# An attention and token-mixer kernel on one core: the first chunk of rows normalised in two halves, v's products of two row blocks first, and identity turns on TensorE until rows arrive

## The chip, the cores and the metric

The kernel runs on one core of one Trainium2 chip. Its engines are TensorE (PE in the profile; PEld is its loading of weights), VectorE (DVE), ScalarE (ACT), GpSimd (POOL) and SyncE (SP), which here issues nearly all DMAs. The metric is the time of one execution on the device in microseconds (us), as the median over runs; lower is better.

## The reference, cut to what matters

`x` has 2048 rows of 512 columns. It is normalised along its rows twice: once for attention, and once more inside the token mixer.

```python
xn = _layernorm(x)
s = _A_ref(xn, A_wqkv, A_wo)                  # 32 heads of 16
g = _silu(_B_ref(xn, B_w1, B_b1, B_w2, B_b2))
return x + s * g

# _A_ref: qkv = x @ wqkv; p = softmax(q k^T * 16 ** -0.5); o = p v; o @ wo
# _B_ref: h = layernorm(x); u = gelu(h^T w1 + b1); y = u w2 + b2; y^T
```

All inputs are float32.

## The kernel before, in words

**Stages.** A first stage normalises x, makes q, k and v, and stores them in DRAM (`q_d`, `k_d`, `v_d`). It takes about 150 us. The rest of the 1700 us goes over the pairs of heads with scores, maxima, exponentials and values, with the mixer's matmuls filled in between. The change lies in the first stage.

**Precision.** Every operand of a matmul is split into an upper part (a copy rounded to `float32r`) and a lower part (the operand less its upper part), and a product is made of three matmuls: upper by upper, upper by lower, lower by upper. The upper part is a copy on ACT, the lower part a subtraction (`sub`, line L79) on DVE where the operand comes out of PSUM, and on POOL for weights and for the second normalisation.

**The first stage.** The 2048 rows are four chunks of four blocks of 128 rows. For a chunk c:

- `load_x` (L165) loads four row blocks; `first(c)` makes a `Norm`: for each block `stats` (L205, L206), then one `rsqrt` for all four (L212 to L218, with the square root on ACT at L213 and one Newton step on DVE), then `apply` for each block (L222), which writes `xn`.
- `turned(c, db)` (L268) transposes column block db of all four row blocks on PE, as a product with the identity `ident`; ACT copies the upper part into `xt` (L270), DVE subtracts for the lower part.
- q and k: eight groups of twelve matmuls (L303), with the weights as the stationary operand and the turned rows moving. ACT copies the upper part of each result (L308) into `sg`, DVE makes the lower part, and SP stores it. Pieces of the next chunk's first normalisation and of this chunk's `second` normalisation (for the mixer, `hx` and `hu`) are put between the groups, in the list `todo`.
- v: for the chunk's four row blocks, twelve matmuls each (L86 to L88), between which the next chunk's rows are turned. ACT copies the result into `v48` (L357), where every head has its 16 columns and 16 ones, and SP stores it (L358).

**Order.** The program's order is written out by hand; each engine takes its instructions in that order, and waits on semaphores are put in from the tiles used. `bank()` hands out the eight PSUM banks in turn. The `xt` tiles come from the pool `pt`, six buffers of one turned column block each.

**Weights.** `wqkv` is loaded in twelve pieces of 128 rows and 512 columns (L185), q's four first, then k's, then v's. There are eleven buffers, so the tenth piece waits until the first is split. `w_upper` (L190) copies the upper parts on ACT, `w_lower` subtracts on POOL. A one-column copy on POOL, `hold` (L280), reads `xn[3]`, so that POOL begins its subtractions when the first chunk's four blocks are normalised.

**Start of the kernel.** The first chunk's normalisation stands alone, with nothing else for PE; the mixer's biases `b1` and `b2` are loaded behind chunk 1's rows (L292, L293), and DVE halves the second (`b2h`, L294) ahead of its work on chunk 0's first q group.

Of the kernel before, what the change touches and what calls it, by code (L numbers as in the profile page):

```python
# [8 lines left out]
F32 = mybir.dt.float32  # L9
F32R = mybir.dt.float32r  # L10
AF = mybir.ActivationFunctionType
OP = mybir.AluOpType
# [9 lines left out]
def tile_attention_token_mixer(ctx, tc, x, wqkv, wo, w1, b1, w2, b2, out):  # L22
    nc = tc.nc
    P = 128
    S, D = x.shape
    F = w1.shape[1]
    DH = 16
    H = D // DH
    NP = H // 2
    NB = S // P  # L30
    ND = D // P
    NF = F // P
    NC = S // 512
# [23 lines left out]
    v_d = dram.tile([NB, P, NP * 48], F32, name="v_d")  # L57
# [6 lines left out]
    ident = const.tile([P, P], F32, name="ident")  # L64
# [13 lines left out]
    def sub(eng, o, a, b):  # L78
        eng.tensor_tensor(out=o, in0=a, in1=b.bitcast(F32), op=OP.subtract)  # L79
# [74 lines left out]
    with (  # L154
        tc.tile_pool(name="pw", bufs=1) as pw,
        tc.tile_pool(name="px", bufs=5) as px,
        tc.tile_pool(name="pt", bufs=6) as pt,
        tc.tile_pool(name="pst", bufs=3) as pst,
    ):
        xr, xn = {}, {}  # L160
# [27 lines left out]
        def w_upper(part):  # L188
            for kd in range(ND):
                nc.scalar.copy(wh[part][:, kd, :], raw_w[part, kd])  # L190

        def w_lower(part):
            for kd in range(ND):
                sub(nc.gpsimd, wl[part][:, kd, :], raw_w[part, kd], wh[part][:, kd, :])

        class Norm:


            def __init__(self, src, dst, then=None):
                self.src, self.dst, self.then = src, dst, then  # L200
# [5 lines left out]
                nc.vector.bn_aggr(self.mv[:, b, :], self.st[:, b, :])  # L206

            def rsqrt(self):
                ve = pst.tile([P, 4], F32, name="ve")
                r = self.r = pst.tile([P, 4], F32, name="r")  # L210
                t = pst.tile([P, 4], F32, name="t")
                nc.vector.tensor_scalar(ve, self.mv[:, :, 1], 1e-5, None, op0=OP.add)  # L212
                nc.scalar.sqrt(t, ve)  # L213
                nc.vector.reciprocal(r, t)
                nc.vector.tensor_tensor(out=t, in0=r, in1=r, op=OP.mult)
                nc.vector.tensor_tensor(out=t, in0=t, in1=ve, op=OP.mult)
                nc.vector.tensor_scalar(t, t, -0.5, 1.5, op0=OP.mult, op1=OP.add)
                nc.vector.tensor_tensor(out=r, in0=r, in1=t, op=OP.mult)  # L218
# [8 lines left out]
                    self.then(b, o)  # L227

            def pieces(self):
                for b in range(4):  # L230
                    yield lambda b=b: self.stats(b)
                yield self.rsqrt
                for b in range(4):
                    yield lambda b=b: self.apply(b)

        def first(c):
# [4 lines left out]
            return Norm(lambda b: xr[4 * c + b], dst)  # L241

        def second(c):
            def then(b, o):
# [8 lines left out]
        def bank():  # L253

            i = turn_of[0] = (turn_of[0] + 1) % 8
            pl, nm = ((ps_sc, "sc"), (ps_mx, "mx"), (ps_dn, "dn"), (ps_av, "av"))[i % 2 if i < 6 else i - 4]
            return pl.tile([P, 512], F32, name=nm)

        for f in first(0).pieces():
            f()  # L260
        w_upper(0)
        xts_ = [[] for _ in range(NC)]

        def turned(c, db):

            ps = bank()
            for b in range(4):
                nc.tensor.transpose(ps[:, b * P : (b + 1) * P], xn[4 * c + b][:, db * P : (db + 1) * P], ident)  # L268
            t = pt.tile([P, 2, 512], F32R, name="xt")
            nc.scalar.copy(t[:, 0, :], ps)  # L270
            sub(nc.vector, t[:, 1, :], ps, t[:, 0, :])
            xts_[c].append(t)

        for c in range(NC):
            cs = slice(c * 512, (c + 1) * 512)
            for db in range(len(xts_[c]), ND):
                turned(c, db)
            if c == 0:

                nc.gpsimd.tensor_copy(pst.tile([P, 1], F32, name="hold"), xn[3][:, :1])  # L280
                w_upper(1)
                w_lower(0)
                w_lower(1)
            xt = xts_[c]
            todo = []
            if c + 1 < NC:
                load_x(c + 1)
                todo += list(first(c + 1).pieces())
            if c == 0:
                w_upper(2)  # L290
                w_lower(2)
                nc.sync.dma_start(b1t, b1.rearrange("(b p) -> p b", p=P))  # L292
                nc.sync.dma_start(b2t, b2.rearrange("(b p) -> p b", p=P))  # L293
                nc.vector.tensor_scalar(b2h, b2t, 0.5, None, op0=OP.mult)  # L294
            todo += list(second(c).pieces())
            order = [(part, g) for part in range(2) for g in range(ND)]
            per = -(-len(todo) // (len(order) + 2))
            for n, (part, g) in enumerate(order):
                m = slice(g * P, (g + 1) * P)
                ps = bank()  # L300
                for w, z in ((wh, 0), (wh, 1), (wl, 0)):
                    for kd in range(ND):
                        nc.tensor.matmul(  # L303
                            ps, w[part][:, kd, m], xt[kd][:, z, :],
                            start=w is wh and z == 0 and kd == 0, stop=w is wl and kd == ND - 1,
                        )
# [33 lines left out]
            pv = [bank()[:, :D] for _ in range(4)]  # L340
            if c + 1 < NC:
                for kd in range(ND):
                    for b in range(4):
# [3 lines left out]
            for b, ps in enumerate(pv):  # L347
                if c + 1 == NC:
                    for kd in range(ND):
                        v_product(b, kd)  # L350
                if c + 1 < NC or b < 2:
                    v48 = pst.tile([P, NP, 3, DH], F32, name="v48", bufs=2)
                else:
                    v48 = pt.tile([P, 2, 512], F32R, name="xt").bitcast(F32).rearrange("p a b -> p (a b)")
                    v48 = v48[:, : NP * 48].rearrange("p (a b c) -> p a b c", b=3, c=DH)
                nc.gpsimd.memset(v48[:, :, 1, :], 1.0)
                nc.scalar.copy(v48[:, :, 0:3:2, :], ps.rearrange("p (a b c) -> p a b c", b=2, c=DH))  # L357
                nc.sync.dma_start(v_d[4 * c + b], v48.rearrange("p a b c -> p (a b c)"))  # L358


    vpp = pool("vp", 2, reuse_waits="tile")
# [689 lines left out]
    ps = two()  # L1051
# [50 lines left out]
```

## Time and profile before

| | us |
|---|---|
| median of 3 runs | 1701.65 |
| lowest and highest | 1699.56, 1702.52 |
| the profiled execution | 1699.51 |
| its span, first to last instruction | 1697.7 |

The prediction below shows lines of the profile. A line of the timeline has the start of an instruction in us from the span's start, how long it took (merged if xN says so), engine, source line, operation, what it writes and reads, its shape, and in brackets how long the engine was idle before it and what ended that. PE rows end in a modelled time, so successive starts tell more than durations. A line of the waits has the waiting instruction, what it waited for, us in total, times, and the longest. A line of the windows has the stretch, its length, the busy time of PE, PEld, DVE, ACT and POOL (with instructions), the granted TensorE clock, the DMA engines' busy share and GB/s.

### The profile page before, as it was taken

How to read it: one execution, taken by the hardware profiler on the slowest of the kernel's cores; microseconds unless marked ns; L12 is line 12 of the kernel's file. 1: busy time of each engine (PE TensorE's matmuls, PEld its weight loads, DVE VectorE, ACT ScalarE, POOL GpSimd, SP SyncE). 2: the span in 40 equal slices, each digit the busy share in tenths (PEclk: the TensorE clock that was granted, in tenths of full speed). 3: DMA queues.
4: the chain of work that ended last, by engine and by line, in shares of the span. 5: the costliest groups of instructions: out<-in, count | busy, mean ns of one | idle time of the engine just before them, and what ended most of it. 6: DMA issues, size and time to landing. Idle time of an engine off the chain costs nothing.

```text
span 1697.7 us, 30716 instructions
## 1 busy us (share of the span) xinstructions
PE 1662.0 (98%) x11693; PEld 842.7 (50%) x11693; DVE 1425.0 (84%) x2476; ACT 1188.0 (70%) x2292; POOL 566.5 (33%) x671
## 2 busy tenths in 40 slices
PE   7999999999999999989999999999999999999997
PEld 6887644444444444444444444444444444444443
DVE  6655998888888888878888888888889988889845
ACT  3332277777777777767777777777777777787764
POOL 3223843234342344323322322222222222372411
PEclk9999999999999999999999999999999999999999
DMA  6568612415150513553241514141412223273345
GB/s 211 186 238 190 131 35 57 73 45 85 45 80 26 92 46 54 148 128 91 60 82 53 92 35 76 35 83 35 66 48 43 52 50 68 82 147 102 116 139 197
DMA packets 151311, 153.72 MB, mean 91 GB/s; under 512 B 51500, under 2 KB 109868, under 8 KB 148092
## 3 DMA queue, kind: packets, MB, share of 16 engines
q1 hardware_dynamic: 146748, 151.02, 37.1%
q8 instruction: 92, 1.51, 0.4%
q0 software_dynamic: 4416, 0.75, 0.3%
q14 instruction: 55, 0.45, 0.1%
HBM read 100.81 MB, written 49.79 MB: 89 GB/s over the span
## 4 chain that ended last, share of the span: by engine, by line
PE 90%; DVE 5%; DMA 2%; ACT 1%; POOL 1%; issue 1%; SPq 0%; DVEq 0%; POOLq 0%
PE av L783 27%; PE dn L921 26%; PE mx L390 13%; PE sc L767 11%; DVE mxp L394 4%; PE dn L896 3%; PE mx L303 2%; PE sc L303 2%; PE av L896 1%; ACT prob L772 1%; PE dn L303 1%; PE av L303 1%; DMA big<-m 1%; PE mx L767 0%; PE sc L86 0%
## 5 line engine op out<-in xcount | busy, mean ns | idle before, releaser
L394 DVE TENSOR_REDUCE mxp<-mx 128x1 f32<-128x512 f32 x2008 | 1248.1, 681 | 164.8 <-PE mx L390 85.1
L772 ACT ACTIVATE prob<-sc 128x512 f32<-128x512 f32 x2008 | 1041.8, 604 | 330.4 <-PE sc L767 269.2
L390 PE MATMUL mx<-big 48*128 48x512 f32 x2008 | 827.7, 428 | 2.6 <-DVE mxp L394 0.8
L767 PE MATMUL sc<-big 50*128 50x512 f32 x2008 | 769.2, 427 | 8.2 <-DMA big<-m 6.7
L921 PE MATMUL dn<-hu,wh 64*128 64x512 f32 x1570 | 573.2, 405 | 0.0
L783 PE MATMUL av<-prob,vp 128*32 128x512 f32 x4096 | 546.0, 605 | 0.0
L390 PEld LDWEIGHTS mx<-big 48*128 48x128 f32 x2008 | 364.0, 186 | 222.3 <-DVE mxp L394 208.1
L767 PEld LDWEIGHTS sc<-big 50*128 50x128 f32 x2008 | 354.5, 185 | 195.2 <-ACT prob L772 170.6
L921 PEld LDWEIGHTS dn<-hu,wh 64*128 64x128 f32 x1570 | 288.7, 185 | 171.8 <-issue 144.9
L921 PE MATMUL dn<-hu,wl 64*128 64x512 f32 x786 | 315.7, 402 | 0.9 <-POOL wl L79 0.9
L148 POOL CAST wh<-raw 128x512 fp32r<-128x512 f32 x108 | 62.9, 583 | 319.3 <-PE dn L921 315.1
L79 POOL TENSOR_TENSOR wl<-raw,wh 128x512 fp32r<-128x512 f32 x124 | 150.4, 1216 | 38.0 <-ACT wh L150 22.7
L783 PEld LDWEIGHTS av<-prob,vp 128*32 128x32 f32 x4096 | 80.9, 108 | 154.9 <-issue 146.5
L921 PEld LDWEIGHTS dn<-hu,wl 64*128 64x128 f32 x786 | 145.6, 185 | 9.4 <-POOL wl L79 1.3
L417 POOL CAST m<-f 16x128 fp32r<-16x128 f32 x32 | 9.0, 280 | 281.2 <-DVE f L406 281.2
L474 POOL TENSOR_TENSOR sq<-u 128x512 f32<-128x512 f32 x14 | 14.6, 1040 | 200.3 <-ACT u L473 200.3
L83 POOL DMA_DIRECT2D big<-m x128 | 66.2, 524 | 0.0
L921 PE MATMUL dn<-wh,hu 64*128 64x512 f32 x132 | 45.7, 399 | 0.0
L79 POOL TENSOR_TENSOR hu<-hx,hu 128x512 fp32r<-128x512 f32 x16 | 20.4, 1290 | 57.1 <-ACT hu L246 57.1
L772 ACT ACTIVATE prob<-mx 128x512 f32<-128x512 f32 x40 | 24.7, 617 | 17.6 <-PE sc L767 9.5
L303 PE MATMUL mx<-xt,big 128*128 128x512 f32 x144 | 35.3, 393 | 0.0
L303 PE MATMUL sc<-xt,big 128*128 128x512 f32 x144 | 34.6, 389 | 0.0
(200 smaller groups left out, 1088.7 us busy)
## 6 DMA issues: line engine op xcount, KB each, us to landing
raw<-in_B_w_dram SPq DMA_DIRECT2D x104, 256.0 KB
big<-k_d SPq DMA_DIRECT2D x96, 128.0 KB
big<-q_d SPq DMA_DIRECT2D x96, 128.0 KB
q_d<-sg SPq DMA_DIRECT2D x16, 512.0 KB
k_d<-sg SPq DMA_DIRECT2D x16, 512.0 KB
num_d<-ev SPq DMA_DIRECT2D x30, 256.0 KB
u_d<-uo SPq DMA_DIRECT2D x14, 512.0 KB
hu<-u_d SPq DMA_DIRECT2D x14, 512.0 KB
```

What stands on the lines that cost most here:

```text
L79: eng.tensor_tensor(out=o, in0=a, in1=b.bitcast(F32), op=OP.subtract)
L83: queue.dma_start(dst.bitcast(F32), src.bitcast(F32))
L148: nc.gpsimd.tensor_copy(whs[n][:, :m, :], raws[n][:, :m, :])
L303: nc.tensor.matmul(ps, w[part][:, kd, m], xt[kd][:, z, :], start=w is wh and z == 0 and kd == 0, stop=w is wl and kd == ND - 1,)
L390: nc.tensor.matmul(ps, q[o : o + 48, r * P : (r + 1) * P], k[o : o + 48, c * 512 : (c + 1) * 512], start=True, stop=True,)
L394: nc.vector.tensor_reduce(mxp[u // 16][:, a, r % 8, c : c + 1], ps, axis=AX.X, op=OP.max)
L474: nc.gpsimd.tensor_tensor(out=sq, in0=u, in1=u, op=OP.mult)
L767: nc.tensor.matmul(ps, ks[p][o : o + 50, kb * P : (kb + 1) * P], qs[p][o : o + 50, at : at + 512], start=True, stop=True,)
L772: nc.scalar.activation(e, ps, AF.Exp, scale=scale)
L783: nc.tensor.matmul(av[32 * j : 32 * j + 32, :], vps[p][:, kb, 16 * a : 16 * a + 32], prob.pop((t, a, c)), start=kb == 0, stop=kb == NB - 1,)
L896: nc.tensor.matmul(ps, w(slice(0, P)), m(slice(0, P)), start=first, stop=last)
L921: made.append(lambda r=r, start=first and a == lead, stop=last and a != lead: nc.tensor.matmul(ps, w(r), m(r), start=start, stop=stop,))
```

## The change

- The first chunk is normalised in two halves of two row blocks, each with its own square root. `Norm` takes the blocks that it is for (`some`), and `rsqrt` is split into `root` and `refine`.
- Until rows arrive, PE transposes the identity 36 times into a PSUM bank that nobody reads (`busy`); 18 more such turns stand between the first products.
- The first chunk's rows are turned by row block (`block_turn`), all four column blocks of a row block into one bank, and copied in two pieces each (`block_upper` on ACT, `block_lower` on DVE).
- v's weights are loaded first, then q's, then k's. v's products of row blocks 0 and 1 come before q's and k's of the first chunk (`v_part`); blocks 2 and 3 follow at the old place.
- `hold` reads `xn[1]`. The lower parts of two of q's weight pieces are made on DVE.
- The results of v's first two blocks are copied and stored ahead of the loads of `b1` and `b2`; their ones are written at the start.
- `pt` has three buffers of two turned column blocks each, where it had six of one.

```diff
-        tc.tile_pool(name="pt", bufs=6) as pt,
+        tc.tile_pool(name="pt", bufs=3) as pt,
...
-        for part in range(3):
+        for n, part in enumerate((2, 0, 1)):
             for kd in range(ND):
-                nm = ("raw", "wh", "wl")[(part * ND + kd) % 3]
+                nm = ("raw", "wh", "wl")[(n * ND + kd) % 3]
...
             def rsqrt(self):
+                self.root()
+                self.refine()
+
+            def root(self):
+                at = slice(self.some[0], self.some[-1] + 1)
...
+                nc.vector.tensor_scalar(ve, self.mv[:, at, 1], 1e-5, None, op0=OP.add)
                 nc.scalar.sqrt(t, ve)
+                self.now = self.r[:, at], t, ve
+
+            def refine(self):
+                r, t, ve = self.now
                 nc.vector.reciprocal(r, t)
...
-        for f in first(0).pieces():
-            f()
-        w_upper(0)
...
+        def block_turn(b):
+            ps = bank()
+            for db in range(ND):
+                nc.tensor.transpose(ps[:, db * P : (db + 1) * P], xn[b][:, db * P : (db + 1) * P], ident)
+            return ps
+
+        def block_upper(b, ps):
+            for h in range(2):
+                nc.scalar.copy(pair[h][:, :, 0, b * P : (b + 1) * P], ps[:, 256 * h : 256 * h + 256].rearrange("p (d q) -> p d q", d=2))
+
+        def block_lower(b, ps):
+            for h in range(2):
+                o = pair[h][:, :, :, b * P : (b + 1) * P]
+                sub(nc.vector, o[:, :, 1, :], ps[:, 256 * h : 256 * h + 256].rearrange("p (d q) -> p d q", d=2), o[:, :, 0, :])
...
+        def busy(n):
+            for _ in range(n):
+                nc.tensor.transpose(idle[:, :P], ident, ident)
+
+        busy(36)
+        one, two = first(0, range(2)), first(0, range(2, 4))
+        for f in one.pieces():
+            f()
...
+        ps0 = block_turn(0)
+        ps1 = block_turn(1)
+        busy(8)
+        two.stats(2)
+        two.stats(3)
+        w_upper(2, [0])
+        block_upper(0, ps0)
+        two.root()
+        w_upper(2, [1])
+        block_lower(0, ps0)
+        nc.gpsimd.tensor_copy(pst.tile([P, 1], F32, name="hold"), xn[1][:, :1])
+        w_lower(2, [0, 1])
+        w_upper(2, [2])
+        block_upper(1, ps1)
+        two.refine()
+        w_upper(2, [3])
+        w_lower(2, [2, 3])
+        for b in (2, 3):
+            two.apply(b)
+        block_lower(1, ps1)
+        for kd in range(ND):
+            v_part(0, 0, wh, [kd])
+            busy((4, 4, 2, 0)[kd])
+        v_part(1, 0, wh, range(ND))
+        v_part(0, 1, wh, range(ND))
+        ps2 = block_turn(2)
+        ps3 = block_turn(3)
+        for b in range(2):
+            v_part(b, 0, wl, range(2))
+        w_upper(0, [0, 1])
+        block_upper(2, ps2)
+        block_upper(3, ps3)
+        w_upper(0, [2, 3])
+        v_part(1, 1, wh, range(ND))
+        block_lower(2, ps2)
+        block_lower(3, ps3)
+        for b in range(2):
+            v_part(b, 0, wl, range(2, ND))
+        w_lower(0, [0, 1])
+        w_lower(0, [2, 3], nc.vector)
...
             if c == 0:
-                w_upper(2)
-                w_lower(2)
+                w_upper(1)
+                w_lower(1)
+                for b in range(2):
+                    v_out(b, pv[b], v48s[b], True)
                 nc.sync.dma_start(b1t, b1.rearrange("(b p) -> p b", p=P))
                 nc.sync.dma_start(b2t, b2.rearrange("(b p) -> p b", p=P))
```

`v_part(b, z, w, kds)` makes the products of row block b's turned columns (z = 0 upper, 1 lower) with v's weights (`wh` upper, `wl` lower) for the pieces kds. `v_out` copies a block's v into its `v48` tile and stores it.

More of the change, by code (lines that the diff above doesn't have):

```diff
@@ L186, in tile_attention_token_mixer, with w_upper, w_lower, __init__ @@
                 raw_w[part, kd] = raw
-        def w_upper(part):
-            for kd in range(ND):
+        def w_upper(part, kds=range(ND)):
+            for kd in kds:
                 nc.scalar.copy(wh[part][:, kd, :], raw_w[part, kd])
-        def w_lower(part):
-            for kd in range(ND):
-                sub(nc.gpsimd, wl[part][:, kd, :], raw_w[part, kd], wh[part][:, kd, :])
+        def w_lower(part, kds=range(ND), eng=nc.gpsimd):
+            for kd in kds:
+                sub(eng, wl[part][:, kd, :], raw_w[part, kd], wh[part][:, kd, :])
         class Norm:
-            def __init__(self, src, dst, then=None):
-                self.src, self.dst, self.then = src, dst, then
+            def __init__(self, src, dst, then=None, some=range(4)):
+                self.src, self.dst, self.then, self.some = src, dst, then, some
                 self.st = pst.tile([P, 4, 6], F32, name="st")
@@ L208, in rsqrt @@
             def rsqrt(self):
[L209 to L212, printed above, removed]
+                self.root()
+                self.refine()
+            def root(self):
+                at = slice(self.some[0], self.some[-1] + 1)
+                ve = pst.tile([P, 4], F32, name="ve")[:, at]
+                self.r = pst.tile([P, 4], F32, name="r")
+                t = pst.tile([P, 4], F32, name="t")[:, at]
+                nc.vector.tensor_scalar(ve, self.mv[:, at, 1], 1e-5, None, op0=OP.add)
                 nc.scalar.sqrt(t, ve)
+                self.now = self.r[:, at], t, ve
+            def refine(self):
+                r, t, ve = self.now
                 nc.vector.reciprocal(r, t)
@@ L229, in pieces, with first @@
             def pieces(self):
-                for b in range(4):
+                for b in self.some:
                     yield lambda b=b: self.stats(b)
                 yield self.rsqrt
-                for b in range(4):
+                for b in self.some:
                     yield lambda b=b: self.apply(b)
-        def first(c):
+        def first(c, some=range(4)):
             def dst(b):
@@ L239, in dst @@
                 return xn[4 * c + b]
-            return Norm(lambda b: xr[4 * c + b], dst)
+            return Norm(lambda b: xr[4 * c + b], dst, some=some)
         def second(c):
@@ L268, in turned @@
                 nc.tensor.transpose(ps[:, b * P : (b + 1) * P], xn[4 * c + b][:, db * P : (db + 1) * P], ident)
-            t = pt.tile([P, 2, 512], F32R, name="xt")
+            if db % 2 == 0:
+                t2 = pt.tile([P, 2, 2, 512], F32R, name="xt")
+                xts_[c] += [t2[:, 0], t2[:, 1]]
+            t = xts_[c][db]
             nc.scalar.copy(t[:, 0, :], ps)
             sub(nc.vector, t[:, 1, :], ps, t[:, 0, :])
-            xts_[c].append(t)
+            done_db[c] = db + 1
@@ new lines, in v_out @@
+        def v_out(n, ps, v48, ones_in=False):
+            if not ones_in:
+                nc.gpsimd.memset(v48[:, :, 1, :], 1.0)
+            nc.scalar.copy(v48[:, :, 0:3:2, :], ps.rearrange("p (a b c) -> p a b c", b=2, c=DH))
+            nc.sync.dma_start(v_d[n], v48.rearrange("p a b c -> p (a b c)"))
+        v48s = [pst.tile([P, NP, 3, DH], F32, name="v48", bufs=2) for _ in range(2)]
+        for v48 in v48s:
+            nc.gpsimd.memset(v48[:, :, 1, :], 1.0)
+        idle = bank()
+        def busy(n):
+            for _ in range(n):
+                nc.tensor.transpose(idle[:, :P], ident, ident)
@@ new lines, in tile_attention_token_mixer, with v_part @@
+        busy(36)
+        one, two = first(0, range(2)), first(0, range(2, 4))
+        for f in one.pieces():
+            f()
+        pair = [pt.tile([P, 2, 2, 512], F32R, name="xt") for _ in range(2)]
+        xts_[0] = [pair[db // 2][:, db % 2] for db in range(ND)]
+        done_db[0] = ND
+        pv = [bank()[:, :D] for _ in range(2)]
+        def v_part(b, z, w, kds):
+            for kd in kds:
+                nc.tensor.matmul(
+                    pv[b], xts_[0][kd][:, z, b * P : (b + 1) * P], w[2][:, kd, :],
+                    start=w is wh and z == 0 and kd == 0, stop=w is wl and kd == ND - 1,
+                )
@@ L274, in tile_attention_token_mixer @@
+        block_lower(3, ps3)
[3 more added lines that the diff above has]
+        w_lower(0, [2, 3], nc.vector)
         for c in range(NC):
             cs = slice(c * 512, (c + 1) * 512)
-            for db in range(len(xts_[c]), ND):
+            for db in range(done_db[c], ND):
                 turned(c, db)
[L278 to L283, printed above, removed]
@@ L338, in v_product @@
                 three(pv[b], xt[kd][:, 0, bs], xt[kd][:, 1, bs], wh[2][:, kd, :], wl[2][:, kd, :], kd == 0, kd == ND - 1)
-            pv = [bank()[:, :D] for _ in range(4)]
+            rest_ = range(2 if c == 0 else 0, 4)
+            pv = {b: bank()[:, :D] for b in rest_}
             if c + 1 < NC:
                 for kd in range(ND):
-                    for b in range(4):
+                    for b in rest_:
                         v_product(b, kd)
@@ L346, in tile_attention_token_mixer @@
                         turned(c + 1, kd + 1)
-            for b, ps in enumerate(pv):
+            for b in rest_:
                 if c + 1 == NC:
@@ L353, in tile_attention_token_mixer @@
                 else:
-                    v48 = pt.tile([P, 2, 512], F32R, name="xt").bitcast(F32).rearrange("p a b -> p (a b)")
+                    if b == 2:
+                        spare = pt.tile([P, 2, 2, 512], F32R, name="xt").bitcast(F32)
+                    v48 = spare[:, b - 2].rearrange("p a b -> p (a b)")
                     v48 = v48[:, : NP * 48].rearrange("p (a b c) -> p a b c", b=3, c=DH)
-                nc.gpsimd.memset(v48[:, :, 1, :], 1.0)
-                nc.scalar.copy(v48[:, :, 0:3:2, :], ps.rearrange("p (a b c) -> p a b c", b=2, c=DH))
-                nc.sync.dma_start(v_d[4 * c + b], v48.rearrange("p a b c -> p (a b c)"))
+                v_out(4 * c + b, pv[b], v48)
     vpp = pool("vp", 2, reuse_waits="tile")
```

1 line of the change is left out of this document (added).

## The prediction

> **What bounds the kernel now.** I read the page's head and chain first, then who TensorE (PE) waited for in the first 170 us, then the timeline of the first 53 us, where all of the change lies.
>
> ```profile
> span 1697.7 us, 30716 instructions
> PE 1662.0 (98%) x11693; PEld 842.7 (50%) x11693; DVE 1425.0 (84%) x2476; ACT 1188.0 (70%) x2292; POOL 566.5 (33%) x671
> PE 90%; DVE 5%; DMA 2%; ACT 1%; POOL 1%; issue 1%; SPq 0%; DVEq 0%; POOLq 0%
> PE mx L268 <- DVE xn L222: 10.2, 1, 10.2
> ```
>
> PE is the chain, and in the first 170 us it has one wait only: 10.2 us for the first normalised rows. What the change can win lies ahead of the first matmul, and whatever is won or lost by the time chunk 1 starts goes to the end of the span, since PE has no wait in the rest of this stage that could take it up.
>
> ```profile
> 1.02 0.29 POOL masks.py:199 TENSOR_SCALAR_AFFINE_SELECT ident<-ident 128x128 f32<-128x128 f32 x1
> 3.50 0.69 DVE L205 BATCH_NORM_STATS2 st<-xr 128x6 f32<-128x512 f32 x1 [2.51 <-DMA xr<-in_A_x_dram]
> 4.32 0.66 DVE L205 BATCH_NORM_STATS2 st<-xr 128x6 f32<-128x512 f32 x1
> 6.25 0.69 DVE L205 BATCH_NORM_STATS2 st<-xr 128x6 f32<-128x512 f32 x1 [1.05 <-DMA xr<-in_A_x_dram]
> 8.00 0.17 DVE L212 TENSOR_SCALAR ve<-mv 128x4 f32<-128x4 f32 x1
> 8.32 0.60 ACT L190 CAST big<-raw 128x512 fp32r<-128x512 f32 x1
> 9.46 1.92 DVE L222 TENSOR_SCALAR xn<-xr,mv,r 128x512 f32<-128x512 f32 x4
> 9.87 0.61 ACT L190 CAST big<-raw 128x512 fp32r<-128x512 f32 x1
> 10.15 1.75 PE L268 MATMUL mx<-ident,xn 128*128 128x128 f32 x4 [10.15 <-DVE xn L222]
> 11.49 0.86 PEld L268 LDWEIGHTS sc<-ident,xn 128*128 128x128 f32 x4
> 14.11 3.33 PE L303 MATMUL mx<-xt,big 128*128 128x512 f32 x12
> 17.28 2.88 PE L303 MATMUL dn<-xt,big 128*128 128x512 f32 x12
> 20.00 2.88 PE L303 MATMUL av<-xt,big 128*128 128x512 f32 x12
> 36.33 0.60 PE L268 MATMUL mx<-ident,xn 128*128 128x128 f32 x4
> 36.65 0.47 PEld L268 LDWEIGHTS dn<-ident,xn 128*128 128x128 f32 x4
> ```
>
> Row blocks 0 and 1 are there at 3.50 and 4.32, block 2 at 6.25; the square root waits for all four. A group of twelve matmuls takes 2.72 us (17.28 to 20.00), 0.227 each. The first group runs from 14.11 to 17.28, so it ends as if it had started, without a gap, at 14.56. The first turns take 0.215 us each (0.86 for four), later ones 0.12 (0.47 for four): PE starts at half rate, and is at full rate when the first group starts, after 4 us of turns alone.
>
> The second bound does not show as a PE wait:
>
> ```profile
> 16.59 4.45 SPq L293 DMA_DIRECT2D b2t<-in_B_b_dram  x1
> 22.81 1.29 POOL L79 TENSOR_TENSOR wvl<-raw,wvh 128x512 fp32r<-128x512 f32 x1
> 23.66 2.96 DVE L294 TENSOR_SCALAR b2h<-b2t 128x16 f32<-128x16 f32 x1 [7.88 <-DMA b2t<-in_B_b_dram]
> 25.30 1.29 POOL L79 TENSOR_TENSOR wvl<-wl,wvh 128x512 fp32r<-128x512 f32 x1
> 26.54 0.68 DVE L79 TENSOR_TENSOR sg<-mx,sg 128x512 fp32r<-128x512 f32 x1
> 26.54:42.46 15.92, 15.92 (x76) 13.22 (x75) 14.76 (x41) 3.12 (x7) 0.05 (x1) 1.00 0.62 232
> 45.06 1.95 DVE L222 TENSOR_SCALAR hx<-xn,mv,r 128x512 f32<-128x512 f32 x2 [1.61 <-POOL hu L79]
> 47.64 0.58 ACT L270 CAST xt<-mx 128x512 fp32r<-128x512 f32 x1
> 49.08 3.14 PE L303 MATMUL mx<-xt,big 128*128 128x512 f32 x12
> 50.05 0.68 DVE L79 TENSOR_TENSOR xt<-sc,xt 128x512 fp32r<-128x512 f32 x1
> 52.05 2.91 PE L303 MATMUL dn<-xt,big 128*128 128x512 f32 x12
> ```
>
> VectorE (DVE) stands 7.88 us for the bias `b2t`, then works without rest from 26.54 to 42.46 (14.76 busy of 15.92), then through the second normalisation's ping-pong with GpSimd (POOL) and ScalarE (ACT) to the copies of chunk 1's turned rows (47.64). The last lower half is done at 50.73; the five matmuls that need it or stand behind it take 1.1, so chunk 1's first group cannot end before 51.9. It ends at 52.05. PE and this DVE chain thus arrive together, and **an earlier PE is worth nothing there unless DVE's chain, which starts with `b2t`, is earlier as well**.
>
> **The change, part by part.** *Halves.* A row's statistics take 0.82 (3.50 to 4.32), so the first half's `ve` comes at 5.2; from `ve` to the first `xn` pass 1.46 (8.00 to 9.46); xn[0] and xn[1] are done at 7.2 and 7.7 (0.48 apart). The second half's statistics follow: its `ve` at 9.35.
>
> *Idle turns.* 36 turns from 1.35. The change to full rate came within 4 us of turning, so some 19 are slow and 17 fast: they end near 7.5, as xn[0] comes. Cost nil; 1.2 us if the rate changes late (1.35 + 32 x 0.215 + 4 x 0.12 = 8.7), and the weights below hide most of that.
>
> *Weights, v first.*
>
> ```profile
> 5.00:10.00 5.00, 0.00 (x0) 0.00 (x0) 3.38 (x13) 1.79 (x5) 0.00 (x0) 1.00 1.02 380
> 50.22 4.39 SPq L358 DMA_DIRECT2D v_d<-v  x4
> 52.66 0.58 ACT L357 COPY v<-mx 128x512 f32<-128x512 f32 x1 [2.02 <-DMA v_d<-v]
> ```
>
> At 380 GB/s a 256 KB piece takes 0.69; x's fourth is in by 7.1, so v's four come at 7.8, 8.5, 9.2 and 9.9. ACT casts them 0.52 apart (8.32 to 9.87 for three steps), but between the first and second it now copies block 0 (until 9.1) and waits for the second `ve`.
>
> *What DVE meets.* In the rows above `b2h`, a tiny operation, stands 2.96 us and ends when POOL's last subtraction does (25.30 + 1.29). The two `hx` take 1.95 where four `xn` take 1.92. So a DVE operation from SBUF to SBUF stands while POOL subtracts. Before, the `hold` kept POOL still until all four rows were normalised; now only until xn[1]. POOL's first lower half runs 8.4 to 9.7, which holds `ve` until 9.7; square root until 10.1; second cast until 10.65; from then POOL has five subtractions ready without a break, 1.25 each (22.81 to 25.30 for two), until 17.0. DVE meanwhile subtracts block 0 (until 10.5) and comes to `refine` and `apply`: three small products, one small `tensor_scalar`, two rows, all from SBUF to SBUF. If one slips in after each POOL operation, xn[2] is done at 17.4 and xn[3] at 18.0; if none does until POOL runs dry, 18.2 and 18.7. The two orders cost about the same.
>
> ```profile
> 102.14 3.98 POOL L79 TENSOR_TENSOR wl<-raw,wh 128x512 fp32r<-128x512 f32 x3 [14.21 <-ACT wh L150]
> 102.18 1.54 DVE L222 TENSOR_SCALAR xn<-xr,mv,r 128x512 f32<-128x512 f32 x1
> ```
>
> Here one does slip in after the first of three. That 128x2 products stand too is not shown by a row; the nearest is `b2h` with 16 columns. The Trainium skill's page "SBUF — State Buffer", section "SBUF: two separate sides", says that VectorE, in a two-port mode or with two SBUF inputs, and GpSimd take one shared port pair by turns, whole instructions at a time. By that rule the small products stand as well, which raises this case's chance.
>
> *PE's path.* Last v cast 12.35 (10.65, 11.2, block 1's copies 0.65, cast), eight matmuls to 14.4, then PE waits for xn[2]; turns of blocks 2 and 3 until 18.5, twelve matmuls (2.7) until 21.2, when q's first group starts. v's 24 matmuls (5.44) are then done: 21.2 - 5.44 = 15.8 against 14.56, so +1.2. Without the wait it is 14.4 + 0.9 + 2.7 = 18.0, so -2.0.
>
> *DVE's path.* SP now issues two `v_d` stores ahead of the biases. ACT: copies of blocks 2 and 3 until 19.5, two q casts and four k casts until 22.65, first v copy until 23.3. Two stores and `b1t` at some 0.46 an issue put `b2t` at 24.7. Its landing has no row that fits. Nearest: 2.4 us from a `v_d` store's issue to the buffer's release (50.22 to 52.66), and 7.1 for `b2t` itself (16.59 to 23.66), then behind four pieces of x. So 27.1 to 31.8. I take 27.8, near the low end, because only two stores (2.1 us together at 380 GB/s) are ahead of it. POOL's k subtractions end at 26.8, so `b2h` then does not stand. DVE starts 1.3 later than 26.54, and chunk 1's first group, less its slack of 0.15, ends 1.15 later. It is about what PE's path gives; the later one counts.
>
> *The rest costs nothing.* Pairs in `pt`: a third turned block waits for kd 1's products instead of kd 0's, but its turns stand behind those on PE anyway. The early `ones` fall into POOL's idle time before 3 us. q's two lower halves on DVE (1.4 us) fit before DVE's wait for `b2t`. Block 7 of x waits for `apply(2)`, and lands near 20, before DVE asks for it.
>
> **Sum.** 1697.7 + 1.2 = 1698.9 of span; the profiled execution took 1699.5 in all, 2.1 below the median of 1701.65. Against the median: **1702.9**.
>
> **Rivals.** *A, DVE is not held* (chance 0.25): small products pass, and rows slip in. Then v's copies are done three microseconds earlier, `b2t` lands near 24.8, DVE is 1.7 early, PE 2.0: -1.7, 1699.9. Against it stands `b2h`.
>
> *B, `b2t` is late* (0.20): it takes its 7.1 us again, so DVE starts at 31.8, 5.3 late, and chunk 1 waits for it: +5.1, 1706.8. It decides from a landing after 27.9, 1.35 later than 26.54, where DVE's path less its slack passes PE's 1.2. The 4.45 us of its issue speak for it, the empty queues at that time against.
>
> *C, idle turns do not raise the rate* (0.05). Then 36 turns end at 9.1 (1.35 + 36 x 0.215), 1.6 later, and the matmuls behind run at half rate for some 4 us, which loses 2 more; a part lies under the wait for xn[2]. About +3, 1704.7. Against it: the first group started at full rate after turns alone. The Trainium skill's page "TensorE: Matmul & The Clock Gate", section "Part 4: PE-mode transpose", says that transposes do not count as busy for the clock; the trace speaks against that.
>
> *D, a wait far from the change goes or stays* (0.10):
>
> ```profile
> 752.71 5.37 DMA big<-m
> 755.00:760.00 5.00, 1.78 (x8) 1.61 (x10) 0.56 (x1) 0.73 (x2) 0.17 (x1) 0.50 1.14 132
> ```
>
> PE waits there for a DMA of 5.37 us, and its clock halves after it. If a shift of a microsecond takes that transfer out of the way, 5 to 8 us go: some 1695.
>
> **Numbers.** The forecast has 0.40. A measurement of this kernel tells 0.2%, 3.4 us, from no change. Faster: D and a fifth of A, 0.15. Slower: B, a fifth of the forecast (a half-rate spell after the 3 us wait) and part of C, 0.30. Same: 0.55. The range leaves out D below and B's worst above: 1698 to 1707; the forecast's own is 1701.5 to 1704.5.
>
> **What would show it.** Right: xn[2] near 17 with `refine` stretched beside POOL's subtractions; a PE gap of some 3 us before block 2's turns; q's first group near 21; `b2h` near 28; chunk 1's first group ending near 53. Wrong: `refine` within 1 us; no PE gap; or `b2h` after 30. Turns at 0.215 beyond 8.2 us would show C.

## The result and the profile after

| | before | after |
|---|---|---|
| median of 12 runs each, us | 1701.59 | 1704.81 |
| lowest and highest, us | 1698.00, 1704.51 | 1702.12, 1705.77 |
| the profiled execution, us | 1699.51 | 1705.29 |
| its span, us | 1697.7 | 1703.5 |

The ratio of after to before is 1.0019, with a 95% interval from 1.0010 to 1.0028: a little slower, and by less than the 0.2% that the prediction took for the bound. The time rose by 3.2 us where 1.2 was forecast.

The page after, its head and its chain by engine:

```profile
span 1703.5 us, 30840 instructions
PE 1672.4 (98%) x11747; PEld 851.9 (50%) x11747; DVE 1430.2 (84%) x2488; ACT 1190.1 (70%) x2297; POOL 564.7 (33%) x669
PE 88%; DVE 6%; DMA 3%; POOL 2%; ACT 1%; issue 1%; SPq 0%; DVEq 0%; POOLq 0%; ACTq 0%
```

PE is still the chain. Its busy time grew by 10.4 us, most of it (8.1, by the timeline's rows) the 54 identity turns in what was a wait. The 10.2 us wait for the first rows is gone from PE's waits in the first 170 us, and in its place stand, beside 1.4 us until the identity is built and 0.7 for casts of v's weights, waits for the normalised rows, the two long ones for the second half's:

```profile
PE dn L289 <- DVE xn L231: 1.4, 1, 1.4
PE av L289 <- DVE xn L231: 0.8, 1, 0.8
PE sc L289 <- DVE xn L231: 0.3, 1, 0.3
```

The timeline after, to the start of DVE's work on the first q group:

```profile
1.36 5.51 PE L316 MATMUL mx<-ident 128*128 128x128 f32 x36 [1.36 <-POOL ident masks.py:199]
7.22 0.66 PE L289 MATMUL sc<-ident,xn 128*128 128x128 f32 x4 [0.34 <-DVE xn L231]
8.27 1.28 POOL L79 TENSOR_TENSOR wvl<-raw,wvh 128x512 fp32r<-128x512 f32 x1 [0.40 <-DMA wh<-in_A_wqkv_dram]
9.26 0.30 DVE L217 TENSOR_SCALAR ve<-mv 128x2 f32<-128x2 f32 x1
10.33 0.16 DVE L224 TENSOR_TENSOR t<-r 128x2 f32<-128x2 f32 x1
10.39 1.28 POOL L79 TENSOR_TENSOR wvl<-wh,wvh 128x512 fp32r<-128x512 f32 x1 [0.84 <-ACT wvh L190]
10.53 1.16 DVE L225 TENSOR_TENSOR t<-t,ve 128x2 f32<-128x2 f32 x1
11.63 1.29 POOL L79 TENSOR_TENSOR wvl<-wl,wvh 128x512 fp32r<-128x512 f32 x1
11.72 1.22 DVE L226 TENSOR_SCALAR t<-t 128x2 f32<-128x2 f32 x1
12.87 1.30 POOL L79 TENSOR_TENSOR wvl<-raw,wvh 128x512 fp32r<-128x512 f32 x1
12.98 1.20 DVE L227 TENSOR_TENSOR r<-r,t 128x2 f32<-128x2 f32 x1
14.22 2.86 DVE L231 TENSOR_SCALAR xn<-xr,mv,r 128x512 f32<-128x512 f32 x2
15.73 0.66 PE L289 MATMUL dn<-ident,xn 128*128 128x128 f32 x4 [1.44 <-DVE xn L231]
17.14 0.66 PE L289 MATMUL av<-ident,xn 128*128 128x128 f32 x4 [0.75 <-DVE xn L231]
21.95 2.90 PE L401 MATMUL sc<-xt,big 128*128 128x512 f32 x12
23.69 1.39 SPq L391 DMA_DIRECT2D b2t<-in_B_b_dram  x1
24.70 2.88 PE L401 MATMUL mx<-xt,big 128*128 128x512 f32 x12
28.35 0.17 DVE L392 TENSOR_SCALAR b2h<-b2t 128x16 f32<-128x16 f32 x1 [7.88 <-DMA b2t<-in_B_b_dram]
28.43 0.68 DVE L79 TENSOR_TENSOR sg<-sc,sg 128x512 fp32r<-128x512 f32 x1
```

Read the DVE rows from 10.33 to 14.22 against the POOL rows. A product on 128x2 elements takes 0.16 us when no subtraction is under way at its start (10.33) and 1.16 to 1.22 beside one, and each ends as a subtraction ends (10.53 + 1.16 = 11.69, 11.63 being the next subtraction's start). PE gets block 2 at 15.73.

The windows after at the start, around that gap, and far behind it:

```profile
1.30:4.10 2.80, 2.73 (x13) 2.74 (x14) 0.66 (x1) 0.72 (x1) 0.51 (x3) 1.00 0.71 243
4.30:7.20 2.90, 2.58 (x24) 2.34 (x22) 2.39 (x11) 0.20 (x1) 0.00 (x0) 1.00 1.02 348
14.30:17.70 3.40, 1.22 (x9) 0.98 (x10) 3.40 (x5) 0.65 (x2) 2.50 (x2) 1.00 0.62 205
17.90:21.20 3.30, 3.30 (x9) 2.59 (x8) 2.46 (x6) 3.30 (x8) 1.09 (x1) 0.50 0.02 5
200.00:216.00 16.00, 14.12 (x70) 9.51 (x70) 12.84 (x22) 6.46 (x12) 15.40 (x16) 0.89 0.39 105
```

In the gap PE is busy 1.22 of 3.40 us, and in the next 3.3 us the granted clock is 0.50: nine matmuls, where two experiments below have 16 and 17 in the same stretch at full clock. (At the start the clock's column shows 1.00 though the turns run at half rate; there the counts, 13 turns and then 24, tell it.)

The timeline after, at chunk 1's first group (the row at 51.11), which answers to the one at 49.08 before:

```profile
41.84 0.69 DVE L79 TENSOR_TENSOR sg<-dn,sg 128x512 fp32r<-128x512 f32 x1 [0.38 <-ACT sg L406]
47.91 1.95 DVE L231 TENSOR_SCALAR hx<-xn,mv,r 128x512 f32<-128x512 f32 x2 [1.60 <-POOL hu L79]
51.11 3.94 PE L401 MATMUL dn<-xt,big 128*128 128x512 f32 x12
52.90 0.68 DVE L79 TENSOR_TENSOR xt<-mx,xt 128x512 fp32r<-128x512 f32 x1
54.90 2.88 PE L401 MATMUL av<-xt,big 128*128 128x512 f32 x12
```

The group is drawn out, 3.94 us against 3.14, because its turned rows' lower halves come one by one until 52.90 + 0.68. Chunk 1's second group starts at 54.90, before at 52.05: **2.85 us late**. This start is the measure of the first stage in all that follows. Nothing of it is won back in the stage: the first maximum (VectorE's first reduction of scores to their maximum, behind the stage, which later expectations go by) starts at 157.16 instead of 154.31, 2.85 late as well. The medians differ by 3.2. That the two profiled spans differ by 5.8 is partly luck: the one before lies 2.1 under its median. It had full clock from 200 to 216 us (0.89 after), but the same 0.89 stands there in profiles of experiments whose median is below the one before.

### The profile page after: what moved, and what is told of

It is laid out like the page before. It is cut to its first block, busy times and chain, and to the rows that moved or that the text cites. A ratio compares the mean times of both kernels' runs of the same rounds, so it can differ in the third digit from the quotient of the medians.

```text
span 1703.5 us, 30840 instructions
## 1 busy us (share of the span) xinstructions
PE 1672.4 (98%) x11747; PEld 851.9 (50%) x11747; DVE 1430.2 (84%) x2488; ACT 1190.1 (70%) x2297; POOL 564.7 (33%) x669
## 4 chain that ended last, share of the span: by engine, by line
PE 88%; DVE 6%; DMA 3%; POOL 2%; ACT 1%; issue 1%; SPq 0%; DVEq 0%; POOLq 0%; ACTq 0%
PE av L882 27%; PE dn L1020 23%; PE mx L489 15%; PE sc L866 12%; DVE mxp L493 4%; PE sc L401 2%; PE mx L401 2%; PE dn L995 2%; PE dn L401 1%; PE av L401 1%; DMA raw<-in_B_w_dram 1%; ACT prob L871 1%; DMA big<-m 1%; DMA big<-k_d 0%; POOL wl L79 0%
```

## The experiments

Every kernel was run in several rounds beside the kernel before on the same chip. "Stage" is the start of chunk 1's second group less the 52.05 of before; "median" is the kernel's less that of the kernel before in the same rounds; the last column has the ratio of the two times with its 95% interval.

| kernel | stage | median | ratio, interval |
|---|---|---|---|
| after | +2.85 | +3.22 | 1.0019 [1.0010, 1.0028] |
| POOL held for four rows | +0.75 | +0.44 | 1.0002 [0.9993, 1.0011] |
| bias halved later | +2.77 | +2.04 | 1.0012 [1.0003, 1.0021] |
| both of these | -0.28 | -0.14 | 0.9998 [0.9989, 1.0007] |
| before, bias halved later | -1.15 | -0.41 | 0.9997 [0.9989, 1.0006] |
| without idle turns | +1.29 | +2.15 | 1.0013 [1.0004, 1.0022] |
| turns in the gap | +1.42 | +2.96 | 1.0023 [1.0014, 1.0033] |
| second normalisation first | +3.52 | +2.94 | 1.0021 [1.0012, 1.0030] |
| before, turns, bias later | -0.93 | -1.13 | 0.9996 [0.9987, 1.0005] |
| both, row passes moved | -1.52 | -1.20 | 0.9994 [0.9986, 1.0003] |
| after, row passes moved | +1.40 | +1.94 | 1.0012 [1.0003, 1.0021] |
| before, turns, bias later, passes moved | -0.87 | -0.03 | 0.9998 [0.9989, 1.0007] |

The stage is from one execution, the median from many; they go together, with up to 1.5 us between them. So the stage tells mechanisms, and a median alone tells apart only what differs by some 2 us.

**POOL held until all four rows are normalised.**

```diff
-        nc.gpsimd.tensor_copy(pst.tile([P, 1], F32, name="hold"), xn[1][:, :1])
-        w_lower(2, [0, 1])
...
-        w_lower(2, [2, 3])
         for b in (2, 3):
             two.apply(b)
+        nc.gpsimd.tensor_copy(pst.tile([P, 1], F32, name="hold"), xn[3][:, :1])
+        w_lower(2)
         block_lower(1, ps1)
```

> The changed kernel, but GpSimd begins its subtractions of weights only when all four row blocks are normalised. Theory (the second half's normalisation stands beside GpSimd's subtractions, PE waits for it and its clock halves after that): refine takes 1 us, xn[3] is done near 12.2 instead of 17.1, PE has no gap before block 2's turns, the clock stays up, q's first group starts near 18.0 instead of 22.0, b2h comes near 25.5 instead of 28.4, and chunk 1's second group starts near 51.0, 3.9 earlier than in the changed kernel and 1.0 earlier than before: about 1700.6 against 1701.6 before. Rival (the late bias alone holds chunk 1): xn[3] and q's first group come earlier all the same, but chunk 1 follows b2h one for one, 2.9 earlier than in the changed kernel, level with before.

**The bias's halving (`b2h`) moved to chunk 2**, in the changed kernel, with the hold above, and in the kernel before:

```diff
                 nc.sync.dma_start(b2t, b2.rearrange("(b p) -> p b", p=P))
+            if c == 2:
                 nc.vector.tensor_scalar(b2h, b2t, 0.5, None, op0=OP.mult)
```

> The changed kernel, but the halving of the bias (b2h) stands in chunk 2 instead of chunk 0, so that VectorE no longer waits for the bias ahead of chunk 0's first q group. Theory (VectorE's chain of chunk 0 is held by the ends of the q and k groups, which are late because q's first group is): VectorE's first subtraction comes at 25.5 instead of 28.4, yet the one of the seventh group stays near 41.8 and chunk 1's second group stays near 55: gain 0 to 0.3. Rival (the late bias holds the chain): chunk 1's second group comes 1.9 to 2.9 earlier, and the time falls by as much.

> Both edits of the two kernels beside it. Theory: q's first group near 18.0, VectorE's first subtraction near 21.5, the seventh group's near 37.8, chunk 1's second group near 50.5: 1.5 earlier than before, some 1700. Rival: the bias held the chain in the first of the two kernels, so this one gains 2 more than that one.

> The kernel before, with the halving of the bias in chunk 2. If VectorE's chain and PE arrive together at chunk 1 (the slack that the prediction read as 0.15), then freeing VectorE 6 us earlier wins only what PE stands at chunk 1's first group: 0.3 to 0.45 us, hardly to be measured in the time but seen as chunk 1's second group starting near 51.7 instead of 52.05. If VectorE alone held it, 2 us or more.

The timeline of the kernel with both edits:

```profile
11.06 1.00 DVE L231 TENSOR_SCALAR xn<-xr,mv,r 128x512 f32<-128x512 f32 x2
18.16 2.23 PE L401 MATMUL sc<-xt,big 128*128 128x512 f32 x9
38.70 0.69 DVE L79 TENSOR_TENSOR sg<-dn,sg 128x512 fp32r<-128x512 f32 x1 [0.37 <-ACT sg L406]
47.99 3.94 PE L401 MATMUL dn<-xt,big 128*128 128x512 f32 x12
51.77 2.89 PE L401 MATMUL av<-xt,big 128*128 128x512 f32 x12
```

With POOL still, both rows of the second half are done at 12.06 instead of 17.08, PE has no gap and keeps its clock, and q's first group starts at 18.16 instead of 21.95 (three of its twelve products then wait until 20.76 for q's last lower half, which POOL now makes later). The hold alone takes 2.1 us off the stage and 2.8 off the median's gap: that DVE stands beside POOL is shown, and that this, with the slow clock that follows the gap, is most of the loss. Chunk 1's second group had been expected near 51.0 with the hold alone and near 50.5 with both edits; it came at 52.80 and 51.77. With both edits, what was missing is found by the last experiment below.

The timeline of the changed kernel with the bias halved later:

```profile
25.43 0.69 DVE L79 TENSOR_TENSOR sg<-sc,sg 128x512 fp32r<-128x512 f32 x1 [4.50 <-ACT sg L407]
41.75 0.69 DVE L79 TENSOR_TENSOR sg<-dn,sg 128x512 fp32r<-128x512 f32 x1 [0.37 <-ACT sg L407]
54.82 2.89 PE L402 MATMUL av<-xt,big 128*128 128x512 f32 x12
```

This went as expected. DVE starts 3.0 us earlier (25.43, not 28.43) and is where it was by the seventh group (41.75, not 41.84), since it then waits for each group's copy. The bias was not what held chunk 1 in the changed kernel. With the hold, where the groups end earlier, it is worth 1.0 of the stage (0.75 to -0.28).

The timeline of the kernel before with the bias halved later:

```profile
48.18 2.88 PE L304 MATMUL mx<-xt,big 128*128 128x512 f32 x12
50.90 2.88 PE L304 MATMUL dn<-xt,big 128*128 128x512 f32 x12
```

Here chunk 1's first group takes 2.72 us to the next one's start, where it took 2.97 before (49.08 to 52.05). So freeing VectorE wins 0.25 there, close to the 0.3 to 0.45 expected; the other 0.9 of the 1.15 was there when PE came to the group, most of it from rows that were ready earlier in this execution.

**Without the idle turns, and with more of them in the gap.**

```diff
-        busy(36)
...
-        busy(8)
...
-            busy((4, 4, 2, 0)[kd])
```

> The changed kernel without any of the turns of the identity (36 ahead and 18 between the products). Theory: PE starts at half rate at 7.2 us and its first products stand apart, so the clock comes up late; v's first twelve products take some 2.7 us more, of which the wait for xn[2] at 15.7 hides a part; q's first group some 1.5 to 3 later than 22.0, chunk 1 as much later, about 1706.5. Rival (the waits for casts and for xn[2] hide all of it, turns are worth nothing): q's first group within 0.5 of 22.0, time within 1 of the changed kernel.

```diff
+        busy(14)
         ps2 = block_turn(2)
+        busy(10)
         ps3 = block_turn(3)
```

> The changed kernel with 14 and 10 more turns of the identity where PE waits for xn[2] and xn[3]. Theory (the half rate from 17.9 to 21.3 comes from the gap, costs 1.7 us there, and turns count as work for the clock): no half-rate spell, q's first group near 20.5 instead of 22.0; VectorE is then held by the bias at 28.4, so that chunk 1's second group comes near 54.0 instead of 54.9. Rival (turns do not count, or the clock drops anyway): the spell stays, q's first group at 22 or later.

The window 17.90 to 21.20 of the kernel without turns, and then of the one with turns in the gap:

```profile
17.90:21.20 3.30, 3.30 (x17) 2.69 (x16) 2.35 (x6) 3.30 (x8) 1.20 (x1) 1.00 0.00 0
```

```profile
17.90:21.20 3.30, 3.30 (x16) 2.71 (x15) 2.34 (x6) 3.30 (x8) 1.09 (x1) 1.00 0.00 0
```

Both keep full clock where the changed kernel had 0.50, and q's first group starts at 20.27 and 20.39, some 1.6 us earlier than in it. That turns fill the gap for the clock is shown by the second. The half-rate spell is no accident of one execution: the kernel "after, row passes moved" of the table keeps the gap, and its profile has the spell too, from 16.70 to 20.00:

```profile
16.70:20.00 3.30, 3.03 (x9) 2.57 (x10) 2.73 (x8) 2.08 (x6) 0.00 (x0) 0.50 0.25 78
```

My theory that the turns are worth something here fell with the first: without them PE's early products are slow, take up the time in which it would wait for rows anyway, and leave too short a gap (PE is busy 2.44 of the 3.40 us from 14.30) for the clock to fall. In the stage the turns even lose 1.56 here (1.29 without them, 2.85 with them). The spell's 1.4 us in the stage did not come back in the second kernel's median (+2.96). Its profiled execution, the slowest of its nine, has a lower clock later (0.81 from 200 to 216 us); whether the others have it too is not known. What the spell is worth over many runs stays open.

**The second normalisation ahead of chunk 1's first one**, on top of both edits, three pieces to a group:

```diff
-            todo += list(second(c).pieces())
+            todo = list(second(c).pieces()) + todo if c == 0 else todo + list(second(c).pieces())
...
-            per = -(-len(todo) // (len(order) + 2))
+            per = 3 if c == 0 else -(-len(todo) // (len(order) + 2))
```

> GpSimd held until four rows are normalised, b2h in chunk 2, and in chunk 0 the pieces of the second normalisation ahead of those of chunk 1's first one, three after each group. Theory (chunk 1's turned copies wait on ACT behind the second normalisation, which stands behind the q and k groups): with these out of the way chunk 1's first group starts when PE comes to it, near 47.5, and the second near 50.2, 1.8 earlier than in the kernel before: about 1699.8. Rival (something else holds chunk 1, such as the stores of q and k): second group at 51.3 as without the reordering.

The waits of PE in that kernel:

```profile
PE sc L274 <- DVE xn L231: 2.5, 2, 1.8
```

This fell too: chunk 1's rows are now late for their turns, and the stage is the worst of all. My reading is that DVE's chain is needed for both, in this order or that; no run separates it from other causes.

**The kernel before with 54 turns ahead and the bias halved later.**

```diff
+        idle = bank()
+        for _ in range(54):
+            nc.tensor.transpose(idle[:, :P], ident, ident)
         for f in first(0).pieces():
             f()
```

> The kernel before with two things alone: 54 turns of the identity ahead of the first chunk, and b2h in chunk 2. Theory: PE is at full rate when the rows come, the sixteen turns take 2 us instead of 4, and q's first group ends near 15.9 instead of 17.3; chunk 1's second group near 50.2, 1.4 for the turns and 0.45 for the bias: about 1699.8. Rival (ACT's copies of the turned rows set the pace, not the turns): q's first group ends within 0.4 of 17.3, and only the bias's 0.45 is won.

Its timeline:

```profile
12.44 3.32 PE L307 MATMUL dn<-xt,big 128*128 128x512 f32 x11
16.28 0.50 PE L307 MATMUL dn<-xt,big 128*128 128x512 f32 x1 [0.52 <-POOL big L79]
51.12 2.88 PE L307 MATMUL av<-xt,big 128*128 128x512 f32 x12
```

The first group starts 1.67 earlier than before (12.44, not 14.11); 0.52 of it goes to a wait for q's last lower half, and 0.93 arrives at chunk 1, where 1.85 had been expected. The edit without the turns brought 1.15, with rows that happened to come 0.7 us earlier in its profile (PE's wait for them is 9.5 instead of 10.2), so the turns' worth is not told apart from chance.

**Four row passes of chunk 0's second normalisation moved to chunk 1's list**, on the kernel with both edits, on the changed kernel, and on the last one above.

```diff
-            todo += list(second(c).pieces())
+            later = list(second(c).pieces())
+            if c == 0:
+                kept, later = later[5:], later[:5]
+            if c == 1:
+                todo = kept[:2] + todo[:2] + kept[2:] + todo[2:]
+            todo += later
```

> The changed order with GpSimd held until all four rows are normalised and the bias's halving in chunk 2, and in addition the four row passes of chunk 0's second normalisation (hx, with their copies and subtractions) moved to chunk 1's list. Theory: the changed order puts half of v's products ahead, so only 24 instead of 48 stand between the last k group and chunk 1's first group, 5.4 us less cover for the second normalisation's ping-pong on VectorE, and that is why chunk 1's first group is drawn out (3.9 us instead of 2.9). Then without these four passes chunk 1's second group starts near 50.3 instead of 51.8, the first maximum comes 1.5 to 1.9 us before that of the kernel before, and the median is 1.5 us or more below it, near 1700.0. Rival: the passes only delay chunk 1's own chain by as much, the first maximum comes 0.3 us before, and the median is about 1701.5.

> The changed kernel with only these four row passes moved to chunk 1's list; GpSimd's hold and the bias as in the change. Theory: of the 2.85 us by which the changed kernel is late at the first maximum, about 1.1 is VectorE's chain through the second normalisation and the rest PE's own lateness (the wait for the rows and the half-rate spell): first maximum 1.7 to 2.0 us later than before, median near 1703.6. Rival: VectorE's chain is nothing but PE's lateness passed on, first maximum 2.8 later, median 1704.8.

> Control: the kernel before with identity turns ahead, the bias's halving in chunk 2, and the same four row passes moved to chunk 1's list. In that order 48 products of v stand ahead of chunk 1's first group, and PE had no wait there without the move. Theory: the move is worth nothing here, first maximum 1.0 us before that of the kernel before, median near 1700.6. Rival: the second normalisation costs here too, first maximum 1.8 us or more before, median near 1699.8.

The timeline of the first of the three, then of the second, then of the third:

```profile
18.07 2.20 PE L406 MATMUL sc<-xt,big 128*128 128x512 f32 x9
47.78 2.90 PE L406 MATMUL dn<-xt,big 128*128 128x512 f32 x12
50.53 2.88 PE L406 MATMUL av<-xt,big 128*128 128x512 f32 x12
```

```profile
21.64 2.88 PE L406 MATMUL sc<-xt,big 128*128 128x512 f32 x12
50.71 2.90 PE L406 MATMUL dn<-xt,big 128*128 128x512 f32 x12
53.45 2.88 PE L406 MATMUL av<-xt,big 128*128 128x512 f32 x12
```

```profile
51.18 2.88 PE L312 MATMUL av<-xt,big 128*128 128x512 f32 x12
```

In both kernels with v's products ahead, chunk 1's first group takes 2.90 instead of 3.94. The stage gains 1.24 and 1.45, of which 0.09 and 0.31 had already been there at q's first group (18.07 against 18.16, 21.64 against 21.95): **1.15 and 1.14 us** by the move. In the order of before it brings nothing (51.18 against 51.12). So the drawn-out group is a price of the changed order: 24 of v's 48 products are gone from between the last k group and chunk 1's first group, 5.4 us less for the second normalisation. By the first maximum the three come 1.52 earlier, 1.40 later and 0.87 earlier than the kernel before, where 1.5 to 1.9 earlier, 1.7 to 2.0 later and 1.0 earlier had been expected. The medians of the two kernels with v's products ahead fall with the move as well (by 1.06 and 1.28), but alone they do not tell it from nothing.

The first of the three has the earliest stage of all, 4.4 us ahead of the changed kernel's. The ratio of its time to the kernel before, 0.9994 [0.9986, 1.0003], lies wholly below the changed kernel's [1.0010, 1.0028]. Against the kernel before, neither it nor the one with turns and the later bias is shown to be faster.

## Why the prediction came out as it did

The forecast was 1702.9; 1704.81 lies within the range, just above the forecast's own 1704.5, and under "within 0.2%". The range was met through the room that it leaves for slower cases: the loss was 3.2 us, not the sum's 1.2. Its main mechanism was found; sizes in it were off, and one step was wrong; the price of the idle turns was in part wrong too.

- **DVE stands beside POOL's subtractions: right.** The small products stand too, as the rule of the Trainium skill's page "SBUF — State Buffer", section "SBUF: two separate sides", has it, and the trace agrees: 1.16 to 1.22 us for what takes 0.16. One operation does pass between two subtractions. Rival A is out: `refine` and its rows took until 17.08 and not 12.06 as with POOL still. But xn[2] came at 15.7, not 17.4: POOL started its second subtraction at 10.39 (I had 10.65), after the first product had passed, so three small operations stood and not four.
- **PE's path: +1.2 foretold, +2.0 measured.** q's second group starts at 24.70, less 5.44 of v's products already done, against 17.28. The gap was 2.2 us rather than 3, so the rows alone would have given q's first group at 20.5 (17.8, when block 3's turns are done, and 2.72), 0.7 under the forecast's 21.2; it came at 21.95, and with turns in the gap at 20.39. The half-rate spell thus cost some 1.5. The prediction named that spell and put it among the slower cases with a fifth of the forecast's chance; it came in the profiled execution, and again where another kernel with the gap was profiled.
- **Idle turns: cost nil ahead of the rows, right; over the whole stage, wrong.** They ended at 6.87, and the rate rose on turns alone: 13 in 2.8 us, then 24 in 2.9. Rival C is out. The sentence of the Trainium skill's page "TensorE: Matmul & The Clock Gate", section "Part 4: PE-mode transpose", that transposes do not count as busy does not hold for these turns of float32; the profile lists them as matmuls with the identity and does not tell whether a transpose mode is on. Without any turns, though, the stage is 1.56 shorter, as the half-rate spell stays away: the prediction priced the turns where they stand, and the gap and the spell elsewhere, and did not join the two.
- **`b2h`: 27.8 foretold, 28.35 measured.** It did not stand (0.17 us), as said; `b2t` landed 4.7 us after its issue began. Rival B, the 7.1 us, is out. The landing did pass 27.9, from which the prediction let the bias decide; that it decided nothing here is shown by the kernel with the bias halved later.
- **The step that was wrong: DVE's chain as one piece that begins with `b2t`.** "An earlier PE is worth nothing there unless DVE's chain, which starts with `b2t`, is earlier as well" took the chain from the first lower half to chunk 1's rows as a rigid shift: 1.3 late at its start, 1.15 late at its end. In the changed kernel it started 1.9 late (28.43) and ended 2.85 late (53.58, not 50.73), while PE came to the group 2.0 late (51.11, not 49.08); and taking `b2t` out changed the next group's start by 0.08. DVE had rests in the later groups, waiting for each group's end on PE, which was now 7.4 us later in the kernel's time (24.70, not 17.28), while chunk 1's rows were wanted only 2 later. The prediction counted v's 24 products as done early and did not ask what they had covered at their old place.
- **The sum** of the stage. By the rows, PE's lateness of 2.0 and 0.8 more for the drawn-out group (3.79 us to the next one's start, 2.97 before). By the runs, 1.4 goes with the spell (turns in the gap) and 1.1 with the lost cover (passes moved). The 0.3 left is what the late rows cost less what the earlier start won; no run has it alone, and single edits need not add up: the hold, which takes out late rows and spell together, took 2.1.
- **Rival D:** the far wait for a DMA stayed, as after's chain of waits shows:

```profile
757.55 5.51 DMA big<-m
```

## What to carry to other kernels

When products are moved ahead to fill an engine's wait, ask what they covered where they stood: here half of v's products were the time in which VectorE finished another job, and the drawn-out group came 30 us after the edit. A long operation on GpSimd given leave to start earlier can hold a chain of tiny VectorE operations at one whole GpSimd operation each; let it start when the chain is through. Trace a late step to the last wait ahead of it, not to the first: `b2t` was a 7.88 us wait in both profiles, and in the changed one it decided next to nothing (0.08 us).

## What the runs showed of the hardware

- The clock fell to half after a stretch in which PE was not idle but busy 1.22 of 3.40 us, and was full again by 21.3 us; the Trainium skill's page "TensorE: Matmul & The Clock Gate", section "What's actually happening", gives a free-running window of about 3.4 us, which agrees with the length of the spell, but lets the clock fall after an idle one, and here a third of it was work. With 24 turns in the gap (busy 3.40 of 3.40) the clock stayed, and so it did in the kernel without idle turns (busy 2.44 of 3.40). Between 1.22 and 2.44 no run here tells.
- A VectorE operation that waits for GpSimd passed at the end of the very operation it met here (10.53 to 11.69), but `b2h` in the kernel before, which came at 23.66, stood through the rest of one and two whole ones more. Why the order differs stays open.
